# One product further ahead: the weight stream of the last block and the preparation of its X operands

## The chip, the core and the metric

One core of one Trainium2 chip runs the whole program. The metric is device time in microseconds. The engines are TensorE (PE in the rows, its weight loads PEld), VectorE (DVE), ScalarE (ACT), GpSimd (POOL) and SyncE (SP), on whose queue nearly all DMAs are issued. Each engine works its own instructions in the order in which the program issues them.

## The reference

A transformer block on S = 2048 rows of D = 576, in float32: attention with 32 heads and one shared key and value head, then a gated bilinear feed-forward part with F = 4608.

```python
x = A_x
h = x + _A_ref(_layernorm(x), wq, wk, wv, wo)
g = jnp.einsum("bsd,df->bsf", xn, w_gate)   # xn = _layernorm(h)
u = jnp.einsum("bsd,df->bsf", xn, w_up)
h2 = h + jnp.einsum("bsf,fd->bsd", g * u, w_down)
```

The last three lines are the part that matters here.

## The kernel before

**Tiling.** The 2048 rows are four blocks of 512 (NB = 4, TB = 512). F is 36 slices of 128 (NF), or 18 pairs of slices (NC). Every float32 operand of a product is kept as two parts, high and low: the high part is a cast of the value to a reduced format, on ScalarE or GpSimd, and the low part is the value less the high part, subtracted on VectorE. A product is then three passes of TensorE: high x high, high x low, low x high.

**The first three blocks.** `ffn(b)` goes over the 36 slices f. For each it forms gate and up products (L932, 54 matmuls on half-height tiles), multiplies them into `hf` (a copy of the gate half on ScalarE, L960, and a product on VectorE, L964), and after every second slice runs `down` for the pair before (L878 to L896). The down products use seven combinations for each 2 x 2 of submatrices, with sums of operands made by `left` (L828) on VectorE and split by `left_sums` (L840). `down` has three PSUM banks for its fourteen stages, so the fourth stage has to wait until VectorE has added the first to the residual (L890).

**The last block's X.** While the third block (b = 2, `end` true) goes over its slices, the generator `ahead()` prepares the normalised rows of the last block, one step at each `next(ahead)`: four normalisations of 128 rows (L994, with a copy on GpSimd, L995); five groups of four transposes (L1002), each copied out of PSUM by ScalarE (L1003); four sums of quarter matrices (L1020 to L1027); ten steps that split nine operands into high and low (L1033 and L1036); and the start of the weight stream. `AHEAD` says at which matmul j of which slice f steps are taken. `TURNS` says how many are taken at once at the end of a slice: in the kernel before after `down` and ahead of g's copy. With the tables before, the normalisations come in slice 29, the transposes after slice 30's down product, sums and splits in slices 31 to 33, the first loads of the stream in slice 34 and its first casts and subtractions in slice 35.

**The last block.** `last_block` goes over 18 turns p. A turn makes both gate and up for a pair of slices by seven products of 256 x 256 operands (`product`, L1143, 12 matmuls each; `tail`, L1150, adds the last 64 of the 576), with stages of `down_pairs` (L1108) for earlier pairs between them, one stage per `go()`. The seven products use seven combinations of X (`XS`, the tiles split by `ahead`) and seven of the weights. The latter stream in: raw values are loaded from DRAM (three straight from the weights, four from sums that GpSimd made during earlier blocks), cast and subtracted, one product's worth per call of `feed`.

**feed(i)** is called after product i. In this order it issues on VectorE the subtraction for product i + 2 (L1062), on ScalarE the cast for product i + 3 (L1065), and on SP the load for product i + LEAD = i + 7 (L1069). The seven operand tiles are `WS` (named wrs, wps, wss and room in the profile, by the memory they lie in). The five raw tiles are a ring, so the load of product i + 7 has to wait for the subtraction of product i + 2. Every seventh call also loads, casts and subtracts the weights of `tail` (`wt`, L1071 to L1078).

**The last quarter.** After product 7p + 6 the turn's last quarter is handled: g is copied (L1242), a12 is a product on VectorE (L1245), S[:, 3] is a difference (L1250), and casts (`high`, L1159, on ScalarE) and subtractions (`low`, L1162, on VectorE) make their parts. Then comes the turn's last feed (L1255), and the next turn begins. `gu11`, `gu12` and `gu22` (L1187, L1206, L1212) are sums on VectorE of PSUM banks; GpSimd multiplies their halves (L1153).

Of the kernel before, what the change touches and what calls it, by code (L numbers as in the profile page):

```python
# [34 lines left out]
NC = NF // 2  # L35
# [22 lines left out]
class Block:  # L58
# [848 lines left out]
    def ffn(self, b):  # L907
        pe, act, dve = self.pe, self.act, self.dve
        X, hid, todo = self.X, [], None
        ahead = self.ahead()  # L910
        if b == 0:
            self.sums = self.weight_sums()
            next(self.sums)
        for f in range(NF):
            n_ = NF * b + f
            k = f % 2
            w = self.ws.pop(n_)
            on = self.more(b + 2)
            last = f == NF - 1 and b + 1 < NB
            end = b == NB - 2  # L920
            if on:
                pg, pu = self.ps_f(f"pg{n_}"), self.ps_f(f"pu{n_}")
            else:
                gu = self.ps_s(f"gu{n_}")
                pg, pu = gu[:, 0], gu[:, 1]
            j = 0
            for c in range(9):
                for wk, xk in ((0, 0), (0, 1), (1, 0)):
                    if on and not last and j % 4 == 0 and self.more(b + 2):
                        self.pair()  # L930
                    for o, ps in ((0, pg), (64, pu)):
                        pe.matmul(ps, w[o:o + 64, wk, c], X[o:o + 64, xk, c], start=(j == 0), stop=(j == 26))  # L932
                    if j == (8 if on else 2) and todo and not plain(n_ - 2):
                        self.left_sums()
                    if j == 3:
                        self.split_w(n_ + 1)
                    if j == 5 and k:
                        self.left_first(n_ - 1, hid[0])
                    if j == 12:
                        self.run_aux(within=True)  # L940
                    if 0 < f < NF - 1 and j in (8, 16, 24) and self.sums:
                        if next(self.sums, "end") == "end":
                            self.sums = None
                            self.load_wd(self.n_wd + 2)
                    if j == 21 and b == f == 0:
                        self.flush(len(self.pend))
                    if j == 6 and last and not end:
                        self.normal(b + 1)
                    if end and f in AHEAD and j in AHEAD[f]:
                        for _ in range(AHEAD[f][j]):  # L950
                            next(ahead)
                    j += 1
            if todo and not on:
                drain(self.down(b, *todo))
                self.load_wd(self.n_wd + 7)
                if end and f in TURNS:
                    for _ in range(TURNS[f]):
                        next(ahead)
            g = self.hh.tile([P, TB], F32, tag="g", bufs=1, name=f"g{n_}")
            act.copy(g, pg)  # L960
            if on and not last and self.more(b + 2):
                self.pair()
            hf = self.hh.tile([P, TB], F32, tag="hf", bufs=2, name=f"hf{n_}")
            dve.tensor_tensor(hf, pu, g, ALU.mult)  # L964
            hid.append(hf)
            if k:
                self.left(n_ - 1, hid)
                hid = []
            self.flush(len(self.pend))
            if todo and on:  # L970
                drain(self.down(b, *todo))
                self.load_wd(self.n_wd + 7)
            if f < NF - 1:
                self.run_aux()
            todo = (f // 2,) if k else None
        if end:
            del X, pg, pu, gu, w, ps, hf, g, self.X
            self.last_block(ahead, self.down(b, *todo))
            return
        both(self.spread(b + 1), self.down(b, *todo))  # L980
        self.load_wd(self.n_wd + 4)
        if b + 2 < NB:
            self.load_x(b + 2)


    def ahead(self):
# [53 lines left out]
        self.raw = self.op.tile([P, 5, TB], F32, tag="ob", name="raw")  # L1040
        self.wt_raw = self.wp.tile([P, 2, 2, P], F32, tag="wor", bufs=1, name="wt_raw")
        for i in range(-LEAD, 0):
            if i == 3 - LEAD:
                yield
                sets = [self.wp.tile([P, 4 * HT], F32R, tag="wr", bufs=2, name=f"wrs{i}") for i in range(2)]
                sets += [self.o_hl.rearrange("p k q -> p (k q)")]
                sets += [self.pp.tile([P, 4 * HT], F32R, tag="P", name=f"wps{i}") for i in range(2)]
                wss = self.wp.tile([P, 2, 4 * HT], F32R, tag="ws", bufs=2, name="wss")
                sets += [wss[:, 0], wss[:, 1]]
                self.WS = [x.rearrange("p (l n) -> p l n", l=2) for x in sets]  # L1050
                self.Wt = self.wp.tile([P, 2, TB], F32R, tag="wos", bufs=1, name="wt")
            self.feed(i)
            if i >= 3 - LEAD:
                yield

    def feed(self, i):

        act, dve, sp = self.act, self.dve, self.sp
        n = i + 2
        if 0 <= n < 7 * NC:  # L1060
            w = self.WS[n % 7]
            dve.tensor_tensor(w[:, 1], self.raw[:, n % 5], f32(w[:, 0]), ALU.subtract)  # L1062
        n = i + 3
        if 0 <= n < 7 * NC:
            act.copy(self.WS[n % 7][:, 0], self.raw[:, n % 5])  # L1065
        n = i + LEAD
        if 0 <= n < 7 * NC:
            m, k = divmod(n, 7)
            sp.dma_start(self.raw[:, n % 5], self.wgs[m, :, (0, 1, None, None, None, None, 2)[k]] if k in (0, 1, 6) else self.wsum_dram[m, :, k - 2])  # L1069
        m, k = divmod(i + 7, 7)  # L1070
        if m < NC:  # L1071
            wt = self.Wt[:, m % 2] if k > 3 else None
            if k == 1:
                sp.dma_start(self.wt_raw, self.wgt[m].rearrange("p f g m -> p (f g m)"))
            if k == 4:
                act.copy(wt, self.wt_raw)
            if k == 5:
                dve.tensor_tensor(wt[64:], self.wt_raw[64:], f32(wt[64:]), ALU.subtract)  # L1078
# [44 lines left out]
    def last_block(self, ahead, D):  # L1123
# [31 lines left out]
        def wide(src):  # L1155
            return src if len(src.shape) == 3 else src.rearrange("p (a q) -> p a q", a=1)

        def high(i, src, n=1):
            act.copy(A[:, 0, i:i + n], wide(src))  # L1159

        def low(i, src, n=1):
            dve.tensor_tensor(A[:, 1, i:i + n], wide(src), f32(A[:, 0, i:i + n]), ALU.subtract)  # L1162

        def go(n=1):
            for _ in range(n):
                next(D, None)

        late = []
        for p in range(NC):
            end = p == NC - 1  # L1170
# [4 lines left out]
            i = 7 * p  # L1175
# [53 lines left out]
            if end:  # L1229
                high(5, a22)  # L1230
                go()
                low(5, a22)
            else:
                low(5, S[:, 2])
                dve.tensor_tensor(S[:, 0], a21, a22, ALU.add)
                high(2, a22)
                dve.tensor_tensor(S[:, 1], S[:, 0], a11, ALU.subtract)
                go()
                high(3, S[:, 0:2], 2)
                low(2, a22)  # L1240
            g = self.hh.tile([P, TB], F32, tag="g", bufs=1, name=f"gl{p}")
            act.copy(g[:, 0:HT], a[:, 0:HT])  # L1242
            if not end:
# [5 lines left out]
            else:  # L1249
# [2 lines left out]
                high(6, S[:, 3])  # L1252
                low(1, a12)
                low(6, S[:, 3])
            self.feed(i + 6)  # L1255
            del hf, a11, a21, a12, a22, g
        drain(D)
        drain(self.down_pairs(b, (NC - 2,)))
# [107 lines left out]
    def run(self):  # L1366
# [15 lines left out]
        with ExitStack() as st:  # L1382
# [91 lines left out]

ORDER = (0, 3, 4, 2, 5, 6, 1)
WD_BUFS = 10
AHEAD = {29: {5: 1, 10: 1, 15: 1, 20: 1}, 31: {2: 1, 5: 1, 8: 1, 11: 1, 14: 1, 17: 1, 20: 1, 23: 1}, 32: {6: 1, 13: 1},
         33: {4: 1, 9: 1, 14: 1, 19: 1}, 34: {10: 1}, 35: {5: 1, 11: 1, 17: 1, 23: 1}}
TURNS = {30: 5}
NAMES = (1, 2, 5, 6, 3, 7, 4)  # L1480
LEAD = 7
QUAD = [(0, P1, True, (0, 0)), (1, P5, True, (1, 1)), (0, P6, False, (0, 1)), (1, P3, False, (0, 1)),
        (0, P7, False, (1, 1)), (0, P4, False, (1, 0)), (1, P2, True, (0, 0))]
ASIDE = (1, 5, 8, 11)
# [9 lines left out]
def both(a, b):  # L1494

    live = [a, b]
    while live:
        live = [x for x in live if next(x, drain) is not drain]


def plain(n):

    return n % NF == NF - 2
# [6 lines left out]
def f32(ap):  # L1510
    return ap.bitcast(F32)
# [15 lines left out]
def drain(gen):  # L1527
    for _ in gen:
        pass
# [85 lines left out]
```

## Time and profile before

| | |
|---|---|
| median of 3 runs | 2349.63 us (2345.38 to 2350.05) |
| the profiled execution | 2346.7 us |
| its span, first to last instruction | 2344.9 us |
| mean granted TensorE clock | 0.993 |
| TensorE, VectorE, ScalarE, GpSimd busy | 97%, 54%, 64%, 30% of the span |
| the last block's 18 turns | about 1961 to 2321 us of the span |

All rows come from one profiled execution. A row of a timeline begins with the start and the length in microseconds, then engine, line, operation, what is written <- what is read, shapes and count; brackets hold the idle time of the engine just before, and what ended it. In rows of one source line three lengths stand as least/median/greatest, in ns. A row of waits ends with the total in us, the number of times and the longest. Granted clock is a share of full speed.

### The profile page before, as it was taken

Reading aid. Unit: us, or ns where it says so; the run is one execution under the profiler, and the core shown is the slowest. Engines: PE = TensorE matmul, PEld = TensorE weight load, DVE = VectorE, ACT = ScalarE, POOL = GpSimd, SP = SyncE. Lnnn points to the kernel's source line nnn. Section 1 sums busy time; section 2 is a strip of 40 time slices with the busy share of each in tenths; the row PEclk is TensorE's granted clock in tenths of the full one; section 3 lists DMA queues with packets and bytes.
Section 4 is the critical chain, followed back from the end, with each engine's and each line's share of the span. In section 5 each row is a group of like instructions: output and inputs, shape, how many; then the busy total and the mean of one; then the engine's idle time right before and its main releaser. Section 6 shows DMA issues by size and latency. Waiting matters only on the chain.

```text
span 2344.9 us, 46338 instructions
## 1 busy us (share of the span) xinstructions
PE 2270.2 (97%) x17958; PEld 1649.9 (70%) x17958; DVE 1272.4 (54%) x2209; ACT 1506.7 (64%) x2046; POOL 714.5 (30%) x826
## 2 busy tenths in 40 slices
PE   7999999999999999999999999999999999898998
PEld 5333345777777777677777777777777878888897
DVE  7555644444445455545454455444444676677665
ACT  6888877767676765676767766676777234444443
POOL 5345301333333323233333333221222332222222
PEclk9999999999999999999999999999999999999999
DMA  5779834545555556555545545543333545666664
GB/s 176 245 258 306 274 136 124 163 155 167 157 171 156 166 158 191 170 167 171 161 160 167 174 151 164 184 147 112 122 127 114 165 139 175 202 206 203 200 216 140
DMA packets 199126, 407.05 MB, mean 174 GB/s; under 512 B 21325, under 2 KB 52941, under 8 KB 198901
## 3 DMA queue, kind: packets, MB, share of 16 engines
q1 hardware_dynamic: 196165, 392.78, 52.4%
q0 software_dynamic: 2736, 11.26, 1.5%
q8 instruction: 143, 2.34, 0.4%
q14 instruction: 82, 0.67, 0.1%
HBM read 317.27 MB, written 74.55 MB: 167 GB/s over the span
## 4 chain that ended last, share of the span: by engine, by line
PE 76%; DVE 7%; ACT 1%; DMA 1%; issue 1%; SPq 0%; DVEq 0%; ACTq 0%
PE pg L932 21%; PE acc L611 15%; PE y L884 13%; PE s L606 9%; PE gs L1143 5%; PE pu L932 4%; PE yq L1108 3%; PE yo L736 2%; PE gu L932 2%; PE gs L1150 1%; DVE wrs L1062 1%; DVE XW L1162 1%; PE y L855 1%; DVE wt L1078 1%; DVE h L1112 0%
## 5 line engine op out<-in xcount | busy, mean ns | idle before, releaser
L607 ACT ACTIVATE P<-s 128x1024 f32<-128x1024 f32 x1024 | 1025.4, 1027 | 282.6 <-PE s L606 202.1
L932 PE MATMUL pu<-X,ws 64*128 64x512 f32 x2565 | 693.7, 389 | 0.0
L932 PE MATMUL pg<-X,ws 64*128 64x512 f32 x2565 | 692.9, 389 | 0.0
L932 PEld LDWEIGHTS pg<-X,ws 64*128 64x128 f32 x2565 | 475.3, 185 | 68.4 <-DMA wsum<-in_wgs_dram 0.8
L611 PE MATMUL acc<-P,V 128*32 128x512 f32 x4096 | 491.3, 599 | 0.7 <-ACT P L607 0.6
L932 PEld LDWEIGHTS pu<-X,ws 64*128 64x128 f32 x2565 | 472.5, 185 | 8.5
L606 PE MATMUL s<-q,kT 56*128 56x512 f32 x2048 | 438.9, 422 | 6.4 <-ACT P L607 3.8
L895 POOL TENSOR_TENSOR h<-h,tmp 128x288 f32<-128x288 f32 x306 | 238.4, 807 | 613.2 <-ACT tmp L894 612.0
L606 PEld LDWEIGHTS s<-q,kT 56*128 56x128 f32 x2048 | 197.8, 184 | 206.1 <-ACT P L607 120.8
L884 PEld LDWEIGHTS y<-wdo,room 128*128 128x128 f32 x2142 | 291.3, 189 | 47.1 <-issue 34.8
L884 PE MATMUL y<-wdo,room 128*128 128x288 f32 x2142 | 304.9, 301 | 5.4 <-DVE h L890 5.3
L611 PEld LDWEIGHTS acc<-P,V 128*32 128x32 f32 x4096 | 114.5, 109 | 247.0 <-issue 234.5
L890 DVE TENSOR_TENSOR h<-h,y 128x288 f32<-128x288 f32 x408 | 175.6, 452 | 200.8 <-PE y L884 200.6
L894 ACT COPY tmp<-y 128x288 f32<-128x288 f32 x306 | 122.1, 399 | 240.9 <-PE y L884 223.5
L964 DVE TENSOR_TENSOR hf<-pu,g 128x512 f32<-128x512 f32 x95 | 65.7, 692 | 302.4 <-ACT g L960 302.4
L92 POOL CAST ws<-wr 128x1152 fp32r<-128x1152 f32 x108 | 126.6, 1173 | 326.5 <-PE pu L932 242.6
L93 DVE TENSOR_TENSOR ws<-wr,ws 128x1152 fp32r<-128x1152 f32 x108 | 181.5, 1680 | 60.8 <-POOL ws L92 59.5
L1091 POOL TENSOR_TENSOR wsum<-wsum,wsum 128x512 f32<-128x512 f32 x72 | 100.4, 1394 | 138.6 <-DMA wsum<-in_wgs_dram 138.4
L93 DVE TENSOR_TENSOR room<-S,room 128x1024 fp32r<-128x1024 f32 x51 | 62.5, 1226 | 133.5 <-ACT room L92 133.5
L1143 PE MATMUL gs<-XS,wrs 128*128 128x256 f32 x432 | 62.6, 287 | 31.8 <-DVE wrs L1062 31.8
L1108 PE MATMUL yq<-wdo,XW 128*128 128x288 f32 x504 | 91.7, 311 | 1.6 <-DVE h L1112 1.6
L1153 POOL TENSOR_TENSOR hfl<-gu 128x256 f32<-128x256 f32 x36 | 33.1, 919 | 170.4 <-DVE gu L1187 156.5
(245 smaller groups left out, 2707.1 us busy)
## 6 DMA issues: line engine op xcount, KB each, us to landing
wdo<-wd_dram SPq DMA_DIRECT2D x492, 288.0 KB
wr<-in_wgu_dram SPq DMA_DIRECT2D x108, 576.0 KB
wsum<-in_wgs_dram SPq DMA_DIRECT2D x108, 256.0 KB
wd_dram<-wd_room SPq DMA_DIRECT2D x20, 1008.0 KB
wsum_dram<-wsum SPq DMA_DIRECT2D x72, 256.0 KB
raw<-wsum_dram SPq DMA_DIRECT2D x72, 256.0 KB
q<-q_dram SPq DMA_DIRECT2D x64, 216.0 KB
raw<-in_wgs_dram SPq DMA_DIRECT2D x54, 256.0 KB
```

Of the source, the lines that this page charges most:

```text
L92: (copy or self.cast)(hi, src)
L93: self.dve.tensor_tensor(lo, src, f32(hi), ALU.subtract)
L606: self.pe.matmul(s_[:, i], self.kT[o:o + 56, t * P:(t + 1) * P], q[o:o + 56, pr], start=True, stop=True)
L607: self.act.activation(p_, s_, AF.Exp, scale=SCALE)
L611: self.pe.matmul(acc[32 * j:32 * j + 32, :], self.V[:, t, :], Ps[j // 2][:, j % 2, :], start=(t == 0), stop=(t == NT - 1), skip_group_chec ...
L884: pe.matmul(y[:, :HD], m[:, t * P:(t + 1) * P], k, start=(first and j == 0), stop=(j == 2), skip_group_check=True)
L890: dve.tensor_tensor(hs, hs, y[:, :HD], ALU.add)
L894: act.copy(z, y[:, :HD])
L895: pool.tensor_tensor(hs, hs, z, ALU.add)
L932: pe.matmul(ps, w[o:o + 64, wk, c], X[o:o + 64, xk, c], start=(j == 0), stop=(j == 26))
L1108: pe.matmul(y[:, :HD], A[:, k, x, t * P:(t + 1) * P], v[:, l], start=(first and z == j == 0), stop=(z == len(pairs) - 1 and j == 2), skip_ ...
L1143: pe.matmul(bank[:, g * HT:(g + 1) * HT], W[:, wk, c, g], X[:, 2 * xk + c], start=(first and g == c == wk == xk == 0), stop=(c == 1 and wk ...
```

## The change

The order of three things is changed; the arithmetic stays the same.

- The stream of weight parts works one product further ahead: after product i, `feed` now subtracts for product i + 3, casts for product i + 4 and loads for product i + 8 (LEAD = 8). `ahead` makes eight calls of feed before the loop in place of seven, four of them at once in slice 34.
- The last feed of a turn stands after the turn's last `low(2, a22)`, ahead of the copy of g and of the last quarter's handling.
- `TURNS` acts after `left` and ahead of `flush`, and no longer behind a down product. The four normalisations are taken at the end of slice 28 and the five groups of transposes at the end of slice 29; the sums and splits are spread over slices 30 to 33 (three, four, three and four steps).

```diff
@@ ffn
             if todo and not on:
                 drain(self.down(b, *todo))
                 self.load_wd(self.n_wd + 7)
-                if end and f in TURNS:
-                    for _ in range(TURNS[f]):
-                        next(ahead)
             g = self.hh.tile([P, TB], F32, tag="g", bufs=1, name=f"g{n_}")
             act.copy(g, pg)
...
             if k:
                 self.left(n_ - 1, hid)
                 hid = []
+            if end and f in TURNS:
+                for _ in range(TURNS[f]):
+                    next(ahead)
             self.flush(len(self.pend))
@@ ahead
         for i in range(-LEAD, 0):
-            if i == 3 - LEAD:
+            if i == 4 - LEAD:
                 yield
...
             self.feed(i)
-            if i >= 3 - LEAD:
+            if i >= 4 - LEAD:
                 yield
@@ feed
-        n = i + 2
+        n = i + 3
         if 0 <= n < 7 * NC:
             w = self.WS[n % 7]
             dve.tensor_tensor(w[:, 1], self.raw[:, n % 5], f32(w[:, 0]), ALU.subtract)
-        n = i + 3
+        n = i + 4
         if 0 <= n < 7 * NC:
             act.copy(self.WS[n % 7][:, 0], self.raw[:, n % 5])
         n = i + LEAD
...
         m, k = divmod(i + 7, 7)
-        if m < NC:
+        if 0 <= m < NC:
@@ last_block
                 high(3, S[:, 0:2], 2)
                 low(2, a22)
+            self.feed(i + 6)
             g = self.hh.tile([P, TB], F32, tag="g", bufs=1, name=f"gl{p}")
             act.copy(g[:, 0:HT], a[:, 0:HT])
...
                 low(6, S[:, 3])
-            self.feed(i + 6)
             del hf, a11, a21, a12, a22, g
@@ tables
-AHEAD = {29: {5: 1, 10: 1, 15: 1, 20: 1}, 31: {2: 1, 5: 1, 8: 1, 11: 1, 14: 1, 17: 1, 20: 1, 23: 1}, 32: {6: 1, 13: 1},
-         33: {4: 1, 9: 1, 14: 1, 19: 1}, 34: {10: 1}, 35: {5: 1, 11: 1, 17: 1, 23: 1}}
-TURNS = {30: 5}
+AHEAD = {30: {4: 1, 10: 1, 16: 1}, 31: {3: 1, 9: 1, 15: 1, 21: 1}, 32: {4: 1, 10: 1, 16: 1},
+         33: {3: 1, 9: 1, 15: 1, 21: 1}, 34: {10: 1}, 35: {5: 1, 11: 1, 17: 1, 23: 1}}
+TURNS = {28: 4, 29: 5}
-LEAD = 7
+LEAD = 8
```

## The prediction

> **What bounds the kernel now.** I read the page first, then the busy time by stretches, then the timelines of TensorE and VectorE in the last block.
>
> ```profile
> span 2344.9 us, 46338 instructions
> PE 2270.2 (97%) x17958; PEld 1649.9 (70%) x17958; DVE 1272.4 (54%) x2209; ACT 1506.7 (64%) x2046; POOL 714.5 (30%) x826
> ...
> L1143 PE MATMUL gs<-XS,wrs 128*128 128x256 f32 x432 | 62.6, 287 | 31.8 <-DVE wrs L1062 31.8
> ```
>
> TensorE is the bound, and it is busy in all but 74.7 us of the span (2344.9 - 2270.2). One row holds 31.8 us of that: the products of the last block (L1143) wait for VectorE's subtraction (L1062) that makes the low part of their weights. The stretches below run from one such wait's end to the next; their columns are length, busy time of PE, PEld, DVE, ACT, POOL, then granted clock, DMA share, GB/s.
>
> ```profile
> 2001.56:2022.53 20.97, 19.32 (x143) 19.11 (x143) 14.19 (x28) 9.33 (x21) 4.52 (x5) 0.92 0.59 186
> 2022.53:2042.44 19.91, 17.80 (x142) 17.59 (x142) 14.04 (x28) 9.34 (x21) 4.52 (x5) 1.00 0.74 226
> ...
> 2083.33:2104.28 20.95, 19.30 (x143) 19.09 (x143) 14.26 (x28) 9.33 (x21) 4.53 (x5) 0.92 0.59 186
> 2104.28:2124.21 19.93, 17.81 (x143) 17.60 (x143) 14.06 (x28) 9.24 (x21) 4.53 (x5) 1.00 0.71 225
> 2287.69:2307.11 19.42, 17.76 (x142) 17.56 (x143) 14.19 (x28) 9.43 (x21) 4.53 (x5) 1.00 0.63 201
> 2022.53:2307.11 284.58, 258.12 (x1988) 255.24 (x1989) 197.80 (x379) 130.27 (x281) 63.36 (x70) 0.96 0.65 206
> ```
>
> Each of these turns of the loop (one p each, 18 in all) holds the same work, 17.80 us of TensorE, and takes 19.4 to 21.0. The turns at clock 0.92 are busy 1.5 us longer for the same instructions. No other engine is full: VectorE has 14.0 to 14.3 us of work in a turn. Where in a turn the wait falls:
>
> ```profile
> 2080.81 0.40 PE L1143 MATMUL gs<-XS,wrs 128*128 128x256 f32 x2
> 2083.33 1.55 PE L1143 MATMUL gs<-XS,wrs 128*128 128x256 f32 x10 [2.12 <-DVE wrs L1062]
> ...
> 2102.23 0.40 PE L1143 MATMUL gs<-XS,wrs 128*128 128x256 f32 x2
> 2104.28 1.46 PE L1143 MATMUL gs<-XS,wrs 128*128 128x256 f32 x10 [1.65 <-DVE wrs L1062]
> 2105.58 0.64 PE L1150 MATMUL gs<-XT_t,wt 128*128 128x256 f32 x4
> ...
> 2106.88 1.60 PE L1143 MATMUL gs<-XS,room 128*128 128x256 f32 x12
> 2108.32 0.56 PE L1108 MATMUL yq<-wdo,XW 128*128 128x288 f32 x3
> 2109.11 1.58 PE L1143 MATMUL gs<-XS,wps 128*128 128x256 f32 x12
> ```
>
> It is the second product of a turn: two matmuls use the high part, the third needs the low part and stands 2.12 or 1.65 us. The queue of VectorE just then, and ScalarE's cast of the same operand:
>
> ```profile
> 2100.84 0.42 DVE L1162 TENSOR_TENSOR XW<-hfl,XW 128x256 fp32r<-128x256 f32 x1
> ...
> 2103.54 0.69 DVE L1062 TENSOR_TENSOR wrs<-raw,wrs 128x512 fp32r<-128x512 f32 x1
> 2104.14 0.45 DVE L1112 TENSOR_TENSOR h<-h,yq 128x288 f32<-128x288 f32 x1
> 2104.50 0.69 DVE L1062 TENSOR_TENSOR room<-raw,room 128x512 fp32r<-128x512 f32 x1
> ```
>
> ```profile
> 2097.76 0.62 ACT L1065 CAST wrs<-raw 128x512 fp32r<-128x512 f32 x1
> ```
>
> The high part was ready at 2098.4, so neither the load nor the cast is late. The subtraction is late because it stands behind the last quarter's handling (the sums S, a12, its low parts), which itself waits for the turn's seventh product.
>
> **The change part by part. First, the stream a product further ahead and before the last quarter.** No instruction of a turn is added or removed: seven subtractions, seven casts, seven loads, only for products one later, and the turn's last feed moves ahead of the copy of g. The second product's low part is then made in the sixth feed, in the place of the row that stood just before the last quarter; the wait at L1143 ends. What is late next: the subtraction that now stands behind the last quarter, for the fourth product of the next turn, in the place of the row at 2104.50, done at 2105.19. Without the wait the fourth product (2109.11 in the trace) starts 1.92 earlier (next paragraph), at 2107.19, and needs the low part two matmuls (0.24) later: 2107.43. The cover is 2.2 us in this turn; where the wait is the longer one VectorE is later by the difference, 2.12 - 1.65, and the cover is 1.8. So I cost the new order at nothing, on VectorE's backlog being worked off before that.
>
> What is removed. A product without a wait takes 1.44 from its start to that of what follows (2106.88 to 2108.32); the one with a 1.65 wait takes 3.35 (2102.23 to 2105.58), so 1.91 to 1.92 are lost, 0.27 more than the idle time the profile shows (the pipeline fills again). The terms: idle time 31.8; refilling, 17 turns x 0.27 = 4.6; the lower clock after a wait, 258.12 - 14 x 17.80 = 8.9 in the fourteen turns of the last stretch row, and 19.32 - 17.80 = 1.5 for the turn from 2001.56, together 10.4. One more wait of the same kind goes:
>
> ```profile
> 1989.84 1.44 PE L1143 MATMUL gs<-XS,wps 128*128 128x256 f32 x10 [0.39 <-DVE wps L1062]
> ...
> 1994.53 1.67 PE L1143 MATMUL gs<-kT,wss 128*128 128x256 f32 x12 [0.88 <-DVE gu L1212]
> ```
>
> The first, 0.39 + 0.27 = 0.7, goes; the second waits for a sum that the change leaves in place, and stays. Sum: 31.8 + 4.6 + 10.4 + 0.7 = 47.5 us. Bounds: all of it; or, if the clock term isn't caused by the waits, 37.1; or, with 1 us a turn coming back at the fourth product, 30.
>
> Of the moved feed every instruction counts. Its cast (0.62) now stands before the copy of g on ScalarE, its subtraction (0.69) before low(3) and a12 on VectorE; behind them a12's own low parts come 0.7 later at most, and their readers on TensorE are stages of the next turns. Its load is passed by no other DMA on SP's queue: the last quarter issues none, so SP only stops waiting earlier. The cast needs a load issued four products before: a turn without its wait is 19.93 - 2.12 - 0.27 = 17.5 us, four sevenths of it 10. The rows for such loads:
>
> ```profile
> 2093.22 3.57 DMA raw<-wsum_dram
> ...
> ACT wt L1076 <- DMA wt_raw<-in_wgt_dram: 1.7, 3, 1.2
> ```
>
> The chain has one at 3.57, and in 15 turns ScalarE waited for a load three times, 1.7 us in all; turns of 17.5 shorten the leads by a seventh. Cost taken 0, at most 0.5 a turn on ScalarE, which TensorE doesn't feel. Before the loop, one more load, cast and subtraction (0.69) move into block 35, where VectorE has idle time; 0.
>
> **Second, X's operands spread.** TensorE's rows around the down products of blocks 28, 30 and 32, and VectorE's before the last of them:
>
> ```profile
> 1884.56 1.75 PE L884 MATMUL y<-wdo,room 128*128 128x288 f32 x9
> 1887.55 4.70 PE L884 MATMUL y<-wdo,room 128*128 128x288 f32 x33 [1.23 <-DVE h L890]
> 1892.17 1.19 PE L932 MATMUL gu<-X,ws 64*128 64x512 f32 x8
> ...
> 1904.64 5.92 PE L884 MATMUL y<-wdo,room 128*128 128x288 f32 x42
> 1910.40 2.67 PE L1002 MATMUL txl<-C,xhl 128*128 128x128 f32 x20
> ...
> 1925.48 1.79 PE L884 MATMUL y<-wdo,room 128*128 128x288 f32 x9
> 1930.31 6.18 PE L884 MATMUL y<-wdo,room 128*128 128x288 f32 x33 [3.04 <-DVE h L890]
> 1936.42 0.96 PE L932 MATMUL gu<-X,ws 64*128 64x512 f32 x6
> ```
>
> ```profile
> 1911.80 2.05 ACT L1003 COPY xtl<-txl 128x512 f32<-128x512 f32 x4 [0.18 <-PE txl L1002]
> ...
> 1914.38 0.69 DVE L964 TENSOR_TENSOR hf<-gu,g 128x512 f32<-128x512 f32 x1 [3.33 <-ACT g L960]
> ...
> 1917.19 0.69 DVE L1022 TENSOR_TENSOR xsums<-xtl,xsums 128x512 f32<-128x512 f32 x1
> 1929.81 0.81 DVE L890 TENSOR_TENSOR h<-h,y 128x288 f32<-128x288 f32 x2
> ```
>
> Block 32's down product takes 1936.42 - 1925.48 = 10.9 instead of the 5.8 of block 30 (1910.40 - 1904.64), as VectorE comes to its adds only at 1929.81. Two things of the change bear on that: the transposes' copies no longer stand in front of g at block 30's end (3.33 idle there), and three sums (3 x 0.69) go to block 30. I take block 28's price for it, 1892.17 - 1884.56 = 7.6, where VectorE comes late by less: 3.3 gained, bounds 0 and 5.1. Against it, the transposes at block 29's end come before ScalarE has emptied the first bank: the copies now follow g's copy, hf and its cast (some 0.6 each by their rows), so the first copy (2.05 / 4) ends 2.4 us after the block and its hand-overs later, while sixteen transposes take 16/20 of 2.67 = 2.1. The fifth group waits; I take 0.8 us. The four normalisations (POOL's copies with them) go before POOL's weight cast of block 29, 2 us late there, but those weights are needed only at block 30. Block 30 then has three sums and a later cast of S before its down product, which has no wait today; VectorE has the block's 6.2 us for it: 0, at most 2 lost. Net 2.5, bounds -2.8 and 5.1.
>
> **Sum.** 47.5 + 2.5 = 50 us. The profiled execution took 2346.7 us around its span of 2344.9, so 2296.7; the median of the three runs shown is 2.9 above it, the lowest 1.3 below. Half of that difference added: 2298.
>
> **The rivals.** (1) *The low clock doesn't come from the waits.* Then 10.4 stay: 2308. For: one wait of 2.12 is followed by a clock of 1.00 (the stretch from 2287.69 above).
>
> ```profile
> 2287.69 1.46 PE L1143 MATMUL gs<-XS,wrs 128*128 128x256 f32 x10 [2.12 <-DVE wrs L1062]
> ```
>
> Against: of the two kinds of wait only the longer is ever followed by 0.92 in these rows (2083.33, and not 2104.28). The Trainium skill ("TensorE: Matmul & The Clock Gate", Part 1: The HAM clock gate (the "warmup" mystery)) says the gate halves the clock after an idle window of about 3.4 us; by that rule waits of 2.12 would not trip it, and the sum would be this rival's. The rows at 0.92 after 2.12 speak against the rule here.
>
> (2) *The wait moves to the fourth product.* VectorE's backlog grows past the 1.8 to 2.2 of cover.
>
> ```profile
> L1062 DVE TENSOR_TENSOR wrs<-raw,wrs x36: 681/689/1224, 1957.2 to 2306.4; 128x512 fp32r<-128x512 f32 x36
> ```
>
> Some subtractions take 1.22 in place of 0.69; it decides once four more of a backlog do. At 1 us a turn, 17 us come back: 2315. Against: the backlog has the same instructions as today.
>
> (3) *The spreading costs.* Block 30's down product waits, block 32's gains nothing: 2.8 lost in place of 2.5 gained, 2303.
>
> (4) *It doesn't do what it says*, since the low part was held by something else: 2348. The cast at 2097.76 excludes the load, and the subtraction's own queue has no idle time before it.
>
> (5) *Slower: ScalarE's cast in front of g waits for its load.* Then g, a12 and all VectorE work behind are late in each turn. It decides once the load is more than 1.8 late (the cover above); to lose the 50 and 5 more, each of 18 turns must lose 3.1, so the load must be 4.9 late, some 15 us after its issue where the chain shows 3.57. Price then 2353.
>
> **How the numbers follow.** Forecast 0.67, rivals 0.1, 0.1, 0.06, 0.03, 0.04. The range goes from 2290 (all of block 32's 5.1 and the lowest run) to 2315, which takes in rivals 1 to 3. A measurement of this kernel can tell about 0.2% (4.7 us) from no change. Faster 0.93, same 0.03, slower 0.04.
>
> **What would show it.** Right: the idle time of L1143 on L1062 near zero, turns of about 17.5 us at clock 1.00, block 32's wait near 1.2. Wrong: waits of L1143 in the fourth product's operand (wps), a clock under 1 without gaps before it, ScalarE's cast waiting on raw, or new waits after L1002. I would be most wrong if VectorE, at 14.2 of 17.5 us, came late at places that the present waits hide.

## The result and the profile after

The changed kernel took 2295.66 us (median of 4 runs, 2294.95 to 2296.35) where the kernel before took 2349.63: a ratio of 0.9774, 95% interval 0.9757 to 0.9791. In a second session it was 0.9783 (0.977 to 0.9796). The profiled execution took 2295.16 us, with a span of 2293.4.

The head of the page, and what the products of the last block waited for (us in total, times; TensorE and its weight loads counted apart):

```profile
span 2293.4 us, 46345 instructions
...
PE 2252.8 (98%) x17958; PEld 1631.7 (71%) x17958; DVE 1268.2 (55%) x2209; ACT 1509.5 (66%) x2046; POOL 713.0 (31%) x826
```

```profile
its engine sat idle before it (us, times) until:
  DVE gu L1212: 1.8, 2
  issue: 0.4, 1
```

The row of 31.8 us that led the prediction is gone from the page: L1143 has no wait for L1062 left. Three turns in a row, in the columns of the earlier stretches:

```profile
2025.04:2042.57 17.53, 17.53 (x145) 17.53 (x144) 14.72 (x29) 9.54 (x20) 4.55 (x5) 1.00 0.77 249
2042.57:2060.09 17.52, 17.52 (x144) 17.52 (x143) 13.42 (x27) 9.35 (x20) 4.54 (x5) 1.00 0.71 229
2060.09:2077.62 17.53, 17.53 (x144) 17.53 (x143) 14.72 (x29) 9.54 (x20) 4.55 (x5) 1.00 0.77 250
```

A turn is 17.5 us, all of it busy, at full clock; before it was 19.4 to 21.0. The second product now runs its twelve matmuls through (2062.32 below), and the subtraction at the place that is late next, 2065.00, ends 1.84 before its reader, two matmuls into the product at 2067.28 (such a distance is called its cover below; in the turn before it is 2.32):

```profile
2062.32 1.59 PE L1143 MATMUL gs<-XS,wrs 128*128 128x256 f32 x12
2063.75 0.64 PE L1150 MATMUL gs<-XT_t,wt 128*128 128x256 f32 x4
...
2065.05 1.60 PE L1143 MATMUL gs<-XS,room 128*128 128x256 f32 x12
2066.49 0.56 PE L1108 MATMUL yq<-wdo,XW 128*128 128x288 f32 x3
...
2067.28 1.58 PE L1143 MATMUL gs<-XS,wps 128*128 128x256 f32 x12
```

```profile
2061.73 0.69 DVE L1062 TENSOR_TENSOR room<-raw,room 128x512 fp32r<-128x512 f32 x1
2062.34 0.69 DVE L1162 TENSOR_TENSOR room<-S,room 128x512 fp32r<-128x512 f32 x1
...
2064.64 0.45 DVE L1112 TENSOR_TENSOR h<-h,yq 128x288 f32<-128x288 f32 x1
2065.00 0.68 DVE L1062 TENSOR_TENSOR wps<-raw,wps 128x512 fp32r<-128x512 f32 x1
```

The slices that prepare X: the wait of the transposes' fifth group, slice 30's down product without a wait, and slice 32's wait (3.04 before):

```profile
1899.68 0.63 PE L1002 MATMUL txl<-C,xhl 128*128 128x128 f32 x4 [0.79 <-ACT xtl L1003]
...
1906.59 5.91 PE L884 MATMUL y<-wdo,room 128*128 128x288 f32 x42
...
1927.67 4.68 PE L884 MATMUL y<-wdo,room 128*128 128x288 f32 x33 [1.33 <-DVE h L890]
```

And one wait of ScalarE that grew (2.5 us in the whole span before), while TensorE stays busy:

```profile
ACT wt L1076 <- DMA wt_raw<-in_wgt_dram: 31.1, 16, 4.2
```

### The profile page after: what moved, and what is told of

Read it like the earlier page. It is cut to its first block, busy times and chain, and to the rows that moved or that the text cites. A ratio compares the mean times of both kernels' runs of the same rounds, so it can differ in the third digit from the quotient of the medians.

```text
span 2293.4 us, 46345 instructions
## 1 busy us (share of the span) xinstructions
PE 2252.8 (98%) x17958; PEld 1631.7 (71%) x17958; DVE 1268.2 (55%) x2209; ACT 1509.5 (66%) x2046; POOL 713.0 (31%) x826
## 4 chain that ended last, share of the span: by engine, by line
PE 83%; DVE 3%; ACT 1%; issue 0%; DMA 0%; SPq 0%; DVEq 0%; ACTq 0%
PE pg L932 21%; PE acc L611 15%; PE y L884 13%; PE s L606 9%; PE gs L1143 8%; PE pu L932 5%; PE yq L1108 4%; PE yo L736 3%; PE gu L932 2%; PE gs L1150 2%; PE y L855 1%; ACT P L607 0%; DVE hf L961 0%; DVE ws L93 0%; ACT room L92 0%
## 5 line engine op out<-in xcount | busy, mean ns | idle before, releaser
L737 DVE TENSOR_TENSOR h<-h,yo 128x288 f32<-128x288 f32 x160 | 65.1, 452 | 33.3 <-PE yo L736 33.2
L932 PE MATMUL gu<-X,ws 64*128 64x512 f32 x702 | 81.9, 389 | 0.0
```

## The experiments

To compare kernels more finely than by whole runs, the table takes the stretch from one event that lies before all edits, the resumption of slice 28's down product after its wait, to the end of the span. That event comes at another time in each execution (1885.94 and 1888.51 in two of the changed kernel, 1887.55 before), so the part ahead of it only adds scatter. All columns behind the ratio are us of the profiled executions; spans are given to 0.1 us.

| kernel | ratio to before (95%) | span | stretch | less than before |
|---|---|---|---|---|
| before | | 2344.9 | 457.35 | |
| changed | 0.9774 (0.9757 to 0.9791) | 2293.4 | 407.46 | 49.89 |
| lead_only | 0.9803 (0.9789 to 0.9816) | 2298.4 | 409.86 | 47.49 |
| front_only | 0.9826 (0.9812 to 0.9839) | 2304.9 | 415.98 | 41.37 |
| spread_only | 0.9987 (0.9978 to 0.9996) | 2342.4 | 455.22 | 2.13 |
| before_plus1 | 1.0019 (1.0007 to 1.003) | 2352.1 | 462.01 | -4.66 |
| before_plus3 | 1.0193 (1.0176 to 1.021) | 2395.6 | 505.83 | -48.48 |
| after_plus4 | 0.982 (0.9803 to 0.9836) | 2301.5 | 414.18 | 43.17 |
| after_plus6 | 0.9889 (0.9872 to 0.9905) | 2319.2 | 429.98 | 27.37 |
| spread_finer | 0.9784 (0.9771 to 0.9797) | 2297.1 | 404.35 | 53.00 |
| changed_again | 0.9783 (0.977 to 0.9796) | 2295.8 | 407.29 | 50.06 |
| finer_again | 0.9785 (0.9772 to 0.9799) | 2293.5 | 405.09 | 52.26 |
| finer_end | 0.9768 (0.9754 to 0.9781) | 2291.9 | 404.32 | 53.03 |

### The three parts alone

**lead_only**: of the diff, the edits of `ahead` and `feed` and LEAD = 8; the last feed, TURNS and AHEAD as before.

> The stream a product further ahead alone: the turn's last feed stays behind the last quarter, and the preparation of X is as before. Theory (the subtraction only had to come out from behind the last quarter): the second product's low part is made one feed earlier, the third product's takes the late place, done 4.2 us after the turn's first product starts where it is wanted at 5.2 (4.93 + 0.24), so no wait is left: 47.5 us less than before, 0.980 of it, clock 1.00 in all turns, idle time of L1143 on L1062 under 2 us. Rival (both halves are needed, since the late place still costs): waits of 0.5 us or more a turn at the third product (room), a gain of 35 us or less.

Measured: 0.9803, and in the stretch 47.49 us less. What L1143 waited for, and the turns together:

```profile
  DVE gu L1212: 1.8, 2
  issue: 0.4, 1
```

```profile
2010.00:2270.00 260.00, 260.00 (x2108) 260.00 (x2108) 209.81 (x401) 139.57 (x296) 66.61 (x74) 1.00 0.72 234
```

No wait for L1062 is left, and in these 260 us TensorE is never idle. The third product's low part ends at 2087.05 in one turn, where it is wanted at 2088.02: a cover of 1.0 us, as expected. The theory holds, the rival falls: the lead alone does it. That the gain agrees to 0.01 is chance, as the spans are known to 0.1 only.

**front_only**: the last feed moved, and nothing else.

```diff
                 low(2, a22)
+            self.feed(i + 6)
             g = self.hh.tile([P, TB], F32, tag="g", bufs=1, name=f"gl{p}")
...
                 low(6, S[:, 3])
-            self.feed(i + 6)
```

> The turn's last feed in front of the last quarter alone, LEAD 7, X as before. Theory: the second product's low part comes in time, the third product's is now made by the next turn's first feed, done 5.2 us after the turn's start (5.7 after the turns that had the longer wait) where 5.2 is wanted: waits of 0 to 0.5 us at the third product (room) in about half the turns, with 0.27 to refill, some 5 us; gain 40 to 45, 0.982 of before. Rival (the two halves only work together): waits near 1 us a turn, gain under 30.

Measured: 0.9826, 41.4 us less in the stretch. The wait is where it was expected, at the third product, in every second turn:

```profile
  DVE room L1062: 6.2, 17
...
2002.04 1.46 PE L1143 MATMUL gs<-XS,room 128*128 128x256 f32 x10 [0.21 <-DVE room L1062]
...
2037.79 1.46 PE L1143 MATMUL gs<-XS,room 128*128 128x256 f32 x10 [0.29 <-DVE room L1062]
```

So either move takes the late subtraction out from behind the last quarter. This one leaves a place with nothing to spare; the lead leaves one with room. Together they gain no more than the lead by itself and the spreading: 47.49 + 2.13 = 49.6 of the changed kernel's 49.9.

**spread_only**: of the diff, TURNS' place, `AHEAD` and `TURNS`; LEAD 7 and the feeds as before.

> X's operands spread alone, the stream and the last quarter as before. Theory: 2.5 us less than before (3.3 at the down product of slice 32, less 0.8 at the transposes), 0.999; the wait before that product's tenth matmul near 1.3 in place of 3.0, the clock there 1.00; the 31.8 us of waits at L1143 stay. Rival (the spreading matters more, as the stream starts from a better state): 5 us or more, and fewer waits at L1143.

Measured: 0.9987, 2.13 us in the stretch. Slice 32's wait, and the waits of L1143:

```profile
1928.91 4.69 PE L884 MATMUL y<-wdo,room 128*128 128x288 f32 x33 [1.34 <-DVE h L890]
```

```profile
  DVE wrs L1062: 67.3, 34
```

The theory's sizes hold, and the state in which the stream starts changes nothing in the waits of the loop: 67.3 here, 67.2 before (TensorE's and its weight loads' added; 31.8 of the 67.2 are TensorE's). Eight turns fell to a low clock here and seven before; in the kernel before a wait behind the turns was followed by a low clock too and here it was not, so that the two about cancel.

### The clock after a wait

Both kernels are the one before, with the turn's last subtraction repeated, once more in before_plus1 and three times more, with range(3), in before_plus3; the same values are written.

```diff
                 low(6, S[:, 3])
+                for _ in range(1):
+                    low(6, S[:, 3])
```

> The kernel before with the last subtraction of the last quarter, low(6, S[:, 3]), issued twice (17 turns, 0.42 us of VectorE each, the same values written again). Theory A (the clock falls after a wait of 2 us or more): the waits of 1.65 become 2.0 to 2.1 and those of 2.12 about 2.5, both kinds of turn fall to clock 0.92; 17 x 0.4 = 7 us for the waits and about 8 x 1.5 = 12 for the clock, 19 us in all, 1.008 of before. Theory B (the low clock goes with something else in every second turn): 7 us, 1.003, the clock in the turns after the shorter wait stays 1.00.

> As before, with that subtraction issued four times in all (three more, about 1.2 us of VectorE a turn). Theory A: waits of 2.8 and 3.3, every turn at a low clock: 17 x 1.2 = 20 us for the waits and 12 or more for the clock, 32 to 40 us, 1.014 to 1.017. Theory B: 20 us, 1.009, and the low clock in every second turn only.

Measured: 1.0019 and 1.0193, or 4.7 and 48.5 us more in the stretch, so neither theory has both sizes. In before_plus1 the waits became 2.12 and 2.59, as both theories had it, yet the clock followed neither. Turns after waits of 2.12, 2.12 and 2.59, in this order:

```profile
2027.48:2049.36 21.88, 19.30 (x142) 19.10 (x142) 14.46 (x29) 9.22 (x20) 4.53 (x5) 0.92 0.66 206
...
2110.95:2131.30 20.35, 17.76 (x143) 17.56 (x143) 14.48 (x29) 9.23 (x20) 4.53 (x5) 1.00 0.69 220
2171.60:2192.97 21.37, 19.25 (x142) 19.04 (x142) 14.61 (x29) 9.43 (x20) 4.53 (x5) 0.92 0.57 182
```

Of its 16 turns from wait to wait, five fell to 0.93 or less, though all but the first followed a wait of 2.12 or more; before, seven did, with shorter waits. In before_plus3, with waits of 3.0 to 3.8, every turn fell, two of them here:

```profile
2032.63:2056.49 23.86, 20.36 (x142) 20.15 (x142) 15.33 (x31) 9.24 (x20) 4.53 (x5) 0.86 0.61 189
2056.49:2079.94 23.45, 20.42 (x143) 20.21 (x143) 15.48 (x31) 9.33 (x20) 4.53 (x5) 0.86 0.51 166
```

So the waits do cause the low clock (without them there is none, with all of them over 3 us there is one each time), but between 2.1 and 2.6 us the length of a wait doesn't decide it. Theory A's threshold in length falls, and so does B, a cause apart from the waits.

What decides is how the wait lies in time. In the turns of all these profiles the granted clock is half for 3.41 us at a time, or for two times 3.41 in a row, and within a profile all such stretches begin on one grid of 3.413 us. Two waits of before_plus1, both 2.12 long (they end at 2069.28 and 2151.21), in windows of this grid, each with the window behind it:

```profile
2065.65:2069.06 3.41, 1.51 (x13) 1.31 (x11) 3.30 (x8) 2.53 (x7) 0.00 (x0) 1.00 0.04 10
2069.06:2072.47 3.41, 3.19 (x15) 3.19 (x16) 1.13 (x3) 0.17 (x1) 0.00 (x0) 0.50 0.59 147
...
2147.57:2150.98 3.41, 1.53 (x13) 1.32 (x11) 3.30 (x8) 2.53 (x7) 0.00 (x0) 1.00 0.01 5
2150.98:2154.39 3.41, 3.18 (x25) 3.18 (x26) 2.28 (x5) 0.56 (x3) 0.30 (x1) 1.00 0.56 150
```

TensorE is idle for 1.90 us of the first window, and the next is at half clock; in the third it is idle for 1.88, and the next is at full clock. In the turns of all thirteen profiles, 37 windows at full clock were followed by one at half clock, and each had 1.90 us of idle time or more; the other 1196 had 1.88 or less. A window at half clock was followed by another one when it held 0.66 us of idle time or more itself (11 times), and by full clock at 0.47 or less. Thus a wait of 2.59 cut in two by the grid did no harm, and the long waits of before_plus3, which reach into a second window, cost more than theory A's 32 to 40. No run moved a wait within its window on purpose.

### The room that VectorE has left

Both kernels are the changed one with the same subtraction repeated in the same way, with range(4) and range(6).

> The changed kernel with low(6, S[:, 3]) issued four times more in each turn (about 1.5 us of VectorE). Theory (VectorE's backlog has a cover of 1.8 us before the fourth product of the next turn): still no wait, within 2 us of the changed kernel, 0.978 of before. Rival (VectorE, at 14 of 17.5 us, has no room left): 1.5 us a turn, 25 us.

> The changed kernel with that subtraction issued six times more (about 2.3 us of VectorE a turn). Theory (cover of 1.8): waits of about 0.4 at the fourth product (wps), with 0.27 to refill some 0.7 a turn, 8 to 14 us over the changed kernel, 0.982 to 0.984 of before. Rival (the cover is larger, or VectorE catches up elsewhere): no wait.

Measured: 6.7 and 22.5 us more than the changed kernel in the stretch. Both expectations miss. Four repeats took 1.85 us, not 1.5 (five in 2.27 below, one in 0.42), and the wait came at another place, the down stage after the third product:

```profile
2033.21 2.27 DVE L1162 TENSOR_TENSOR XW<-S,XW 128x256 fp32r<-128x256 f32 x5
2035.40 0.45 DVE L1112 TENSOR_TENSOR h<-h,yq 128x288 f32<-128x288 f32 x1
```

```profile
2033.97 1.60 PE L1143 MATMUL gs<-XS,room 128*128 128x256 f32 x12
2035.90 0.66 PE L1108 MATMUL yq<-wdo,room 128*128 128x288 f32 x3 [0.33 <-DVE h L1112]
```

```profile
PE yq L1108 <- DVE h L1112: 15.8, 16, 1.2
```

The first four rows are of after_plus4, the last is of after_plus6. That stage waits for the add (L1112) of the stage two steps earlier, which has the same tile of PSUM banks, and this add is the first thing behind the last quarter. In the changed kernel it ends at 2065.09 (2064.64 + 0.45, above) and the stage starts at 2066.49: a cover of 1.40 in such turns (1.88 in the others), less than the 1.84 of the fourth product. Repeats of 1.85 less 1.40 leave 0.45. In every second turn of after_plus4 the stage starts 1.93 after its product (2035.90 - 2033.97) in place of 1.44 (2066.49 - 2065.05), 0.49 late, of which the profile shows 0.33 as idle. The first turns also waited once at the fourth product (0.98 and 1.91 us).

### What could still be had

**spread_finer** and **finer_again** are one kernel: TURNS' steps ahead of `left`, and other numbers of steps a slice.

```diff
             hid.append(hf)
+            if end and f in TURNS:
+                for _ in range(TURNS[f]):
+                    next(ahead)
             if k:
                 self.left(n_ - 1, hid)
                 hid = []
-            if end and f in TURNS:
-                for _ in range(TURNS[f]):
-                    next(ahead)
...
-AHEAD = {30: {4: 1, 10: 1, 16: 1}, 31: {3: 1, 9: 1, 15: 1, 21: 1}, 32: {4: 1, 10: 1, 16: 1},
+AHEAD = {30: {4: 1, 10: 1, 16: 1}, 31: {3: 1, 7: 1, 11: 1, 15: 1, 19: 1, 23: 1}, 32: {16: 1},
```

> The changed kernel with the TURNS steps moved ahead of left (so that ScalarE's five copies stand before the cast of hf) and the steps of slices 30 to 33 as 3, 6, 1, 4 in place of 3, 4, 3, 4. Theory (the two waits left there are the copies' place in ScalarE's queue, and VectorE's subtractions of slice 32 ahead of its adds): the 0.79 at the transposes and the 1.33 at slice 32's down product go, with 0.3 to refill: 2.4 us under the changed kernel in the span, 0.976 of before. Rival (the work only moves): slice 31 or slice 30 gets a wait of the same size, no gain.

> The changed kernel once more, beside the next two on one chip, as their measure: 0.977 to 0.979 of before.

> The finer spreading once more beside the changed kernel. Theory (its first profile was 3.1 us shorter from slice 28's down product to the end, and lost that in the start-up of the kernel by chance): the stretch from the resumption in slice 28's down product to the end is 404.3 again, against 407.5; medians 2 to 4 us under the changed kernel, if the start-up doesn't hide it. Rival: the gain was a chance of one execution, no difference.

The wait at the transposes is gone, slice 32's is 0.23:

```profile
1928.06 4.68 PE L884 MATMUL y<-wdo,room 128*128 128x288 f32 x33 [0.23 <-DVE h L890]
```

In the stretch that is 404.35 and 405.09 against the changed kernel's 407.46 and 407.29: 2.2 to 3.1 us, where 2.4 was expected. Whole runs don't show it (0.9785 and 0.9783 in one session, medians 1.3 us apart where 2 to 4 were expected); the first profile lost 6.8 us before the stretch began (1892.75 against 1885.94).

**finer_end** adds one edit in `down_pairs`.

```diff
-                if 2 * i + t not in ASIDE:
+                if 2 * i + t not in ASIDE + ((13,) if pairs[0] == NC - 4 else ()):
```

> The finer spreading, and at the end of the last block the last add of the pairs 14 and 15 (the stage after the seventh product of the last turn) taken by ScalarE and GpSimd in place of VectorE. Theory (the wait of 1.26 before the last pair's down products is a bank held by that add, which stands behind the last quarter on VectorE): the 1.26 goes, with 0.27 to refill, 1.5 us under the finer spreading in the stretch. Rival (the bank is held by an earlier add, or ScalarE is as late): no gain, or the wait is put down to ScalarE's copy.

The rival holds. The wait near the end stays, 1.33 where it was 1.26, and the add that ends it (2272.33) is still VectorE's:

```profile
2272.33 0.45 DVE L1112 TENSOR_TENSOR h<-h,yq 128x288 f32<-128x288 f32 x1
...
2272.83 1.05 PE L1108 MATMUL yq<-wdo,XW 128*128 128x288 f32 x6 [1.33 <-DVE h L1112]
```

The add that was moved isn't the one that holds the bank. It has the lowest median of the session, and its five runs (2291.51 to 2294.34) all lie below the changed kernel's five (2295.75 to 2297.59), though the intervals of the ratios overlap (0.9754 to 0.9781 and 0.977 to 0.9796). The runs of the finer spreading alone reach from 2293.30 to 2301.33, and in the stretch the two are the same (404.32 against 404.35 and 405.09). So a gain of some 3 us over the changed kernel is likely, and which of the edits gives it in whole runs isn't shown.

## Why the prediction was right, step by step

**The sum of the stream** was 47.5 us; lead_only gained 47.49 in the stretch. Its terms were idle time, refilling, clock and one wait of 0.39. L1143's waits for L1062 went to zero, so the idle time and its refilling went, and the clock of the loop is 1.00. Refilling and clock can be read apart against the changed kernel's 17.53 a turn. A turn of the kernel before at full clock that ends with a wait of 2.12 takes 19.92, 0.27 more than both together: the refilling. One at 0.92 that ends with a wait of 1.66 takes 20.97: without 17.53, 1.66 and 0.27, 1.51 are left for the clock, where the prediction had 1.5.

**The waits cause the low clock**: rival 1 falls. The rows after waits of 1.65 and 2.12 had seemed to give a length from which the clock falls; before_plus1 shows that this reading was too simple. The wait of 2.12 that spoke for the rival (2287.69) lay across two windows of the grid, with 1.77 us in the later one.

**What is late next** is the step that was incomplete. The prediction named the fourth product's subtraction, with a cover of 1.8 to 2.2 us; after the change its cover was 1.84 in the turn shown. But a shorter one, 1.40, lay at the stage after the third product, by way of PSUM and an add (L1112), and the prediction did not see it. Neither is used up, so the time didn't show the miss; the repeated subtractions did. Rival 2 in its deciding point was thus nearer than it looked.

**Both moves were costed as one.** The prediction gave the gain to lead and order together. The lead alone has all of it, the order alone 41.4.

**The spreading** was 3.3 gained at slice 32 and 0.8 lost at the transposes, 2.5 in all. Slice 32's wait fell from 3.04 to 1.33, and the 33 matmuls behind it from 6.18 to 4.68: 3.2 in all. The loss was 0.79 at the transposes, 1.06 with 0.27 to refill. That leaves 2.15; the net was 2.13 alone and 407.46 against 409.86, or 2.40, on top of the lead. That the loss came out at 0.79 is luck: the rows gave 0.3 (2.4 less 2.1), and the rest of the 0.8 was an allowance. Rival 3 falls: the down product of slice 30, where the three sums went, had no wait (1906.59).

**The loads** were taken to cost ScalarE at most 0.5 us a turn. ScalarE waited 31.1 us for `wt`, 1.7 a turn: the size was wrong by more than three times. That TensorE doesn't feel it was right, as it has no idle time in the turns. Rival 5 would have needed a wait at the cast in front of g (L1065), and that line waits for nothing in the changed kernel.

**The total**: 50 us off the profiled 2346.7 gave 2296.7, and the profiled execution took 2295.16. The 1.3 us added for the median of before were not needed. Of the 51.5 us between the two profiles 49.89 lie in the stretch; the other 1.6 come before any edit and are chance.

## What to carry to other kernels

Where an engine works several streams in one in-order queue, look at which instruction stands behind the longest chain, and let it serve something that is due later; one step more of lead can be worth as much as a better order or more (47.5 against 41.4 us here), and the order may then be left alone. Before such a change, list every reader of what comes next behind that chain, among them accumulators that have to be read before they are written again, and not only the stream that was late. A stretch of the trace from an event that all versions share differed by 0.2 and 0.7 us between two profiles of one kernel here, while the time ahead of it differed by 2.6 and 4.3.

## What the runs showed of the hardware

A wait of TensorE costs more than its idle time (0.27 us more at full clock, and some 1.5 on top where the clock falls), and how much depends on when it falls. In spread_only the ten matmuls after the waits of 2.12 to 2.14 us take less time from one such wait to the next:

```profile
2039.43 2.50 PE L1143 MATMUL gs<-XS,wrs 128*128 128x256 f32 x10 [2.12 <-DVE wrs L1062]
...
2161.98 2.25 PE L1143 MATMUL gs<-XS,wrs 128*128 128x256 f32 x10 [2.14 <-DVE wrs L1062]
...
2284.51 1.97 PE L1143 MATMUL gs<-XS,wrs 128*128 128x256 f32 x10 [2.13 <-DVE wrs L1062]
```

These waits come every 40.85 us ((2284.51 - 2039.43) / 6), the windows at half clock every 40.96 ((2285.19 - 2039.43) / 6):

```profile
2039.43:2042.84 3.41, 3.41 (x16) 3.41 (x17) 0.92 (x2) 0.41 (x1) 0.00 (x0) 0.50 0.47 157
...
2285.19:2288.60 3.41, 3.41 (x18) 3.41 (x17) 1.39 (x3) 0.00 (x0) 0.32 (x1) 0.50 0.47 154
```

So the slow part begins a little later behind each wait, on a grid that runs on its own. The Trainium skill ("TensorE: Matmul & The Clock Gate", Part 1: The HAM clock gate (the "warmup" mystery)) describes such a window, free-running and 3413 ns long; twelve of them are 40.96 us, 0.11 more than two turns, which is the drift seen here. The same section has the clock fall after an idle window; here the measurement says less is enough. In the turns 1.90 us of idle time in one window of 3.41 were enough, so that waits of 2.12 us and more took the clock down in seven of eight cases before, and those of 1.65 never did.

Idle time in a window is not the whole rule. At the wait of 1.26 us near the end of the kernel, behind the turns, windows with 1.42 to 1.61 us of idle time were followed by half clock in eight profiles, and one with 1.39 was not. What is different there stays open.
